# Handing out the late gathers at the planner's own end, two more PSUM banks for odd transform halves, and expert activations laid over the tables

## The chip, the cores and the metric

The kernel runs on one core of one Trainium2 chip. The metric is device time in microseconds (us) of one execution; lower is better. The engines are named as the profile names them: PE (TensorE matmul), PEld (its weight loads), DVE (VectorE), ACT (ScalarE), POOL (GpSimd) and SP (SyncE, which only issues DMAs here).

## The reference

The input `x` has 8 batches of 2496 tokens with 256 values. The first half is the real part of a Fourier transform over tokens and values. The second half sends each of the 19968 rows of that result to one of eight experts, each of which takes at most N // E = 2496 rows, in the order of falling gate values, and applies the expert's two layers.

```python
X = np.fft.fft(np.fft.fft(x, axis=1), axis=2).real.astype(np.float32)
x = X.reshape(B * S, D)                      # N = 19968 rows, D = 256
logits = x @ w_gate                          # E = 8 experts
for idx in np.argsort(-logits.flatten()):    # greedy: highest logit first
    tok, e = idx // E, idx % E
    if assigned[tok] < 0 and counts[e] < N // E:
        assigned[tok] = e; counts[e] += 1
for e in range(E):                           # F = 1024 hidden values
    out[assigned == e] = np.maximum(x[assigned == e] @ w1[e], 0.0) @ w2[e]
```

## The kernel before, in words

The work runs in four stages on one core, and the order of the instructions on PE, DVE, ACT and POOL is the order in which the program emits them (`manual_schedule`).

**Loading and folding.** Rows are loaded, folded with their mirror image and turned; cosine and sine tables `hi` and `lo` are made in the pool `tabs`; the gate's logits come out of the same tables.

**Transforms.** `transform(n)` runs for n = 0 to 19, in two units each: the even half (r = 0), which ACT copies to `ev`, and the odd half (r = 1). A `combine` then adds and subtracts the two on DVE into a stage buffer, ACT and POOL fill in the mirrored quarters, and SP stores the buffer to `t_dram`. The combine of transform n is kept in the list `pending` and emitted in the even unit of transform n + 1. Both halves take their PSUM from `big_ps`, three banks of the tag `h`, which the weight products `wps` (`turn_w`) and the sort products `sps` (`sort_call`) use as well. Two more banks have the tags `t` and `o`; until the experts start, only `first_strips` and the row sums use them. Between the units runs `first_chain`: the first search for the gate's thresholds (`choose`, `lowest`, `search`, `first_strips`), on DVE with short products on PE. It fixes early strips of rows that surely belong to an expert. A small clock (`clock["PE"]`, `clock["D"]`) decides how many units are emitted between two steps of the chain.

**Experts.** `experts` runs iterations j over 40 early tiles (5 strips by 8 experts, 384 rows) and 16 late tiles (8 experts by two). Iteration j has three parts; each emits a third of `up` of tile j (first layer, `hps` to the hidden tile `hb`, L1218) and a third of `down` of tile j - 1 (second layer, `ops`, L1241, then a scatter to the output by POOL, L1245). PSUM results are moved by `take`, which gives each move to ACT or DVE by the running sums `busy`. The list `aside` holds further steps for a part: weights, sort marks, sort products, reloads.

**Rounds.** Beside the early tiles runs `settle_rest`, the rest of the assignment: the end of round 1, three more rounds (each `choose`, `lowest`, three turns of `search`, `settle`), then slots, keys, eight chunks of `inverse` and `decode`, which gives the row numbers of the late tiles. It is a generator: each `yield` names the DVE time of what was just emitted, and `yield SYNC` marks a place where a product on PE follows. At the end of each part `pace` adds 1.9 to its credit, never above 1.9, and emits steps until the credit is spent or a SYNC comes. `place_all`, at iteration 25 part 1, emits all that is left at once. The gathers of the late tiles (POOL, L1194) are put at fixed iterations, 25 + 3m // 2 for late tile m and not before 32 from m = 8 on. When `settle_rest` has ended, `swap_ps` gives the banks of the rounds to the experts, and `widen` gives the buffers `wa` and `dd` to the ring of output tiles.

When the transforms are done, `swap_sb` closes the pool of the stage buffers (`stg`) and that of the tables (`tabs`), which lie next to each other, and opens one pool `deep` over both, for the hidden tiles `hb`, the odd strips `xs`, the gathered rows `xg`, their turned copies `xt` and a ramp `ramp8`.

If the rounds left a token unsettled, a fallback runs after the experts.

Of the kernel before, what the change touches and what calls it, by code (L numbers as in the profile page):

```python
# [52 lines left out]
CB = 20  # L53
KC = 64
OT = 8
SYNC = None
MARK = 1048576.0

# [9 lines left out]
def kernel(  # L68
# [424 lines left out]
    def big_ps(nm):  # L493
        return spread_ps("h", 3, [P, 512], FT, nm)
# [12 lines left out]
    def swap_sb():  # L507
        stg_cm.__exit__(None, None, None)
        tabs_cm.__exit__(None, None, None)
        deep["sb"] = ctx.enter_context(tc.tile_pool(name="deep", bufs=1, side="right"))  # L510

    def work_tile(shape, dt, tag, bufs):
        return deep["sb"].tile(shape, dt, tag=tag, bufs=bufs, name=tag)


    wa = asg.tile([P, E, GC], FT, name="wa")
# [284 lines left out]
        nc.vector.tensor_tensor(kk, kk, none, op=AL.add)  # L801
        nc.vector.scalar_tensor_tensor(rows, in0=bb, scalar=float(S // 2), in1=kk, op0=AL.mult, op1=AL.add)

    ramps = {}
# [12 lines left out]
    def first_strips():  # L817
        low, wid, lo0 = found["low"], found["wid"], found["lo0"]
        lev = small("lev")
        nc.vector.scalar_tensor_tensor(lev, in0=wid, scalar=-0.01, in1=low, op0=AL.mult, op1=AL.add)  # L820
        moved = small("moved")
        nc.vector.tensor_tensor(moved, low, lo0, op=AL.is_gt)
        nc.vector.tensor_scalar(moved, in0=moved, scalar1=2.0 * T_FREE, scalar2=-T_FREE, op0=AL.mult, op1=AL.add)
        fits = small("fits")
        nc.vector.tensor_scalar(fits, in0=exc, scalar1=0.5, scalar2=2.0 * T_FREE, op0=AL.is_lt, op1=AL.mult)
        nc.vector.tensor_scalar(fits, in0=fits, scalar1=-T_FREE, scalar2=None, op0=AL.add)
        nc.vector.scalar_tensor_tensor(lev, in0=lev, scalar=moved, in1=fits, op0=AL.min, op1=AL.max)
        yield 0.8
        yield SYNC
        bps = psm.tile([P, 512], FT, tag="o", bufs=1, name="lev_ps")  # L830
        nc.tensor.transpose(bps[:, 0:P], lev.to_broadcast([P, P]), identf)
# [7 lines left out]
        yield SYNC  # L839
        v = asg.tile([P, GC], FT, tag="sl_v", bufs=1, name="sl_v")  # L840
# [24 lines left out]
        yield 5.5  # L865
        early["t"] = (v, t1, t2, t3)

    def strip_places():
# [125 lines left out]
    td_v = t_dram.rearrange("(n p f) d -> n p f d", p=P, f=8)  # L994
    NB = 2

    pending = []

    def transform(n):
        b0, kc = NB * (n // NK), n % NK  # L1000
        ks = slice(kc * P, (kc + 1) * P)
        st = stg.tile([P, NB, 4, D], BF, tag="stage", bufs=4, name="stage")
        ps = []
        for r in range(2):
            fps = big_ps("fftps").rearrange("p (b d) -> p b d", b=NB)
            for d0, d1, tab in ((0, P + 1, hi["c" + "EO"[r]]), (P + 1, D, hi["s" + "EO"[r]])):
                for i in range(NK):
                    nv = rows_of(i, r)
                    nc.tensor.matmul(fps[:, :, d0:d1], lhsT=tab[:nv, i, ks],  # L1009
                                     rhs=zball[:nv, b0:b0 + NB, 2 * i + r, d0:d1],  # L1010
                                     start=(i == 0), stop=(i == NK - 1))
            ps.append(fps)
            if r == 0:
                ev = stg.tile([P, NB, D], FT, tag="ev", bufs=2, name="ev")
                nc.scalar.copy(ev, fps)  # L1015
            cost = 0.0
            while pending:
                cost += pending.pop(0)()
            yield cost

        def combine():
            nc.vector.tensor_tensor(st[:, :, 0, :], ev, ps[1], op=AL.add)  # L1022
            nc.vector.tensor_tensor(st[:, :, 3, :], ev, ps[1], op=AL.subtract)  # L1023
            for q in range(2):
                nc.scalar.activation(st[:, :, 1 + q, P + 1:D], st[:, :, 3 * q, P + 1:D], ACT.Copy, bias=0.0,  # L1025
                                     scale=-1.0)
                nc.gpsimd.tensor_copy(st[:, :, 1 + q, 0:P + 1], st[:, :, 3 * q, 0:P + 1])  # L1027
            nc.sync.dma_start(td_v[n].rearrange("p f d -> p (f d)"), st.rearrange("p b q d -> p (b q d)"))
            if n < 3:
                reload(n)  # L1030
            return 1.3

        pending.append(combine)


    def turn_w(e, eng=None):
# [105 lines left out]
        clock["D"] = max(clock["D"], clock["PE"]) + 0.3  # L1142
        clock["PE"] = max(clock["D"], clock["PE"])
    for n in range(4):
        sort_mark(n)
        unit()
        sort_call(n, (0, 1), "A")
        unit()
        sort_call(n, (2, 3), "A")
        unit()  # L1150
        reload(n + 3)
        if n == 0:
            strip_places()
        if n == 1:
            payloads(0, payr)
    sort_rows(0, 0)
    while unit():
        pass
    while pending:
        pending.pop(0)()  # L1160
    swap_sb()
    ramp8 = deep["sb"].tile([P, P, 8], BF, name="ramp8")
    ramps[8] = ramp8
    nc.gpsimd.tensor_copy(ramp8, rampw[:, 0:P, None].to_broadcast([P, P, 8]))
    busy["A"] = busy["D"] = 0.0
# [85 lines left out]
    def experts(tiles, group, aside, ahead=0, pace=None):  # L1251
# [4 lines left out]
        for j in range(len(tiles) + 1):  # L1256
            if ahead and j + ahead < len(tiles):
                gather(tiles[j + ahead])
            for part, (fcs, b0) in enumerate((((0, 1, 2), 0), ((3, 4, 5), P), ((6, 7), 2 * P))):
# [6 lines left out]
                if j > 0:  # L1266
                    down(tiles[j - 1], b0, group)
                if pace is not None:
                    pace()
# [12 lines left out]
    for t in range(1, NT):  # L1282
# [6 lines left out]
                at(j + 1, 2, lambda n=n: reload(n + 3))  # L1289
        at(8 * t - 4, 1, lambda t=t: sort_rows(t, 0))  # L1290
        at(8 * t - 1, 0, lambda t=t: sort_rows(t, 1))
    G0 = 25
    for m, d in enumerate(late):
        d["m"] = m
        j = G0 + (3 * m) // 2 if m < 5 else max(32, G0 + (3 * m) // 2) if m >= 8 else G0 + (3 * m) // 2
        at(j, 1, lambda d=d: (place_all(), gather(d)))

    todo = settle_rest()
    placed = []
# [82 lines left out]
```

## Time and profile before

| what | us |
|---|---|
| median of 3 runs | 612.94 |
| lowest and highest of them | 610.62 and 614.84 |
| the profiled execution, its own time | 607.89 |
| its span, from the first to the last instruction | 606.0 |

The profile describes the one execution of 607.89 us. Its page gives busy time per engine, the span in 40 slices, and the chain of work that ended last. The trace behind it answers further questions: busy time in chosen stretches (with the clock that TensorE was granted, 1.00 being full speed), who waited for whom, and instructions in order of time. In rows of the stretches each engine's busy time has its count of instructions in brackets. In rows of the timeline the bracket at the end is the engine's idle time before the instruction and what ended it. In rows of waits the numbers are the total in us, how often, and the longest.

### The profile page before, as it was taken

The numbers are of one execution on the slowest core, as the hardware profiler recorded it, in microseconds if no ns is written. First come the engines' busy times: TensorE is split into PE (matmuls) and PEld (weight loads), VectorE is DVE, ScalarE is ACT, GpSimd is POOL, SyncE is SP. The second block draws the span as 40 slices with busy tenths as digits, with TensorE's granted clock in tenths as the row PEclk, the third lists the DMA queues.
The fourth block names the chain that finished last, engine by engine and source line by source line (L and its number), as shares of the span: only waits on it lengthen the run. The fifth ranks groups of instructions, "written<-read, shape, count | busy, mean of one in ns | idle before, by whom it ended". The sixth has DMA issues, their size and how long they took to land.

```text
span 606.0 us, 11341 instructions
## 1 busy us (share of the span) xinstructions
PE 491.7 (81%) x4023; PEld 363.0 (60%) x4023; DVE 391.4 (65%) x1074; ACT 340.7 (56%) x775; POOL 314.6 (52%) x362
## 2 busy tenths in 40 slices
PE   0577688886978999998999987889687679768994
PEld 0444447755755667776776765557455456556773
DVE  7799865958584878989679898335324234334551
ACT  7889851553656877876777762335323234334551
POOL 7888541622314544644444443566674665665554
PEclk9998999999897999998999997889997898997998
DMA  8999762684697984222222321122221221221111
GB/s 278 305 281 298 226 101 41 222 260 125 164 298 133 165 156 144 98 98 84 96 95 85 94 93 62 55 67 65 73 64 59 65 73 55 58 69 47 60 65 48
DMA packets 35169, 74.63 MB, mean 123 GB/s; under 512 B 6115, under 2 KB 14349, under 8 KB 35104
## 3 DMA queue, kind: packets, MB, share of 16 engines
q0 software_dynamic: 23296, 42.10, 27.3%
q1 hardware_dynamic: 11808, 31.73, 15.7%
q8 instruction: 33, 0.54, 0.4%
q14 instruction: 32, 0.26, 0.1%
HBM read 51.26 MB, written 32.24 MB: 138 GB/s over the span
## 4 chain that ended last, share of the span: by engine, by line
PE 62%; DVE 16%; issue 10%; ACT 8%; POOL 2%; another core or an unknown queue 1%; DMA 1%; POOLq 0%; DVEq 0%; ACTq 0%; SPq 0%
PE hps L1218 22%; PE ops L1241 20%; PE fftps L1009 4%; PE sps L1082 3%; PE tp L284 3%; PE wps L1042 2%; POOL out_dram L1245 2%; DVE pt L1060 2%; ACT zt L286 1%; PE yps L294 1%; DVE stage L1023 1%; PE tp L1206 1%; ACT tf L253 1%; DMA t_dram<-stage 1%
## 5 line engine op out<-in xcount | busy, mean ns | idle before, releaser
L985 ACT ACTIVATE hb<-hps 128x384 bf16<-128x384 f32 (+1 forms) x331 | 147.5, 491 | 93.0 <-PE hps L1218 68.4
L1241 PE MATMUL ops<-w2t,hb 128*128 128x256 bf16 (+1 forms) x1344 | 183.1, 282 | 0.8 <-issue 0.8
L1241 PEld LDWEIGHTS <-hb 128*128 128x128 bf16 (+1 forms) x1344 | 136.5, 102 | 38.5 <-issue 4.3
L1218 PE MATMUL hps<-xs,zball 128*128 128x384 bf16 x640 | 136.9, 341 | 27.3 <-issue 16.6
L1245 POOL DMA_INDIRECT out_dram<-zball,rid x95 | 98.6, 1038 | 109.5 <-ACT zball L985 88.8
L1218 PEld LDWEIGHTS <-zball 128*128 128x128 bf16 x896 | 88.5, 101 | 93.1 <-issue 54.7
L989 DVE TENSOR_SCALAR hb<-hps 128x384 bf16<-128x384 f32 (+1 forms) x117 | 63.3, 547 | 78.0 <-PE hps L1218 43.3
L1218 PE MATMUL hps<-xt,zball 128*128 128x384 bf16 (+1 forms) x256 | 51.3, 330 | 14.6 <-issue 10.7
L128 POOL DMA_INDIRECT xb<-in_x_dram,mir_i x40 | 55.2, 1380 | 11.9 <-issue 11.1
L985 ACT ACTIVATE zball<-ops 128x256 f32<-128x256 f32 x86 | 33.1, 384 | 36.3 <-PE ops L1241 23.5
L284 PE MATMUL tp<-identf,xa 128*128 128x128 f32 x160 | 27.5, 336 | 21.0 <-issue 12.2
L985 ACT ACTIVATE xs<-sps 128x384 bf16<-128x384 f32 x71 | 31.6, 489 | 20.0 <-PE hps L1218 11.3
L284 PEld LDWEIGHTS tp<-identf,xa 128*128 128x128 f32 x160 | 23.2, 174 | 28.6 <-issue 13.1
L1027 POOL COPY stage<-stage 128x258 bf16<-128x258 bf16 x40 | 17.6, 444 | 39.0 <-DVE stage L1022 35.8
L1082 PE MATMUL sps<-pt,xl 128*128 128x192 bf16 x320 | 34.6, 248 | 1.2 <-DVE stage L1023 0.7
L991 DVE COPY zball<-ops 128x256 f32<-128x256 f32 (+1 forms) x32 | 13.5, 423 | 33.3 <-PE ops L1241 12.5
L1060 DVE TENSOR_SCALAR pt<-rampw,spot 128x193 bf16<-128x193 bf16 x160 | 32.4, 294 | 0.0
L1194 POOL DMA_INDIRECT xg<-t_dram,ids_l x24 | 23.5, 978 | 14.9 <-DVE wa L781 7.9
L1082 PEld LDWEIGHTS <-xl 128*128 128x128 bf16 x320 | 28.0, 99 | 4.5 <-issue 1.4
L1245 POOL DMA_INDIRECT out_dram<-zball,rows_l x23 | 22.3, 970 | 15.2 <-DVE zball L991 7.6
L1015 ACT COPY ev<-fftps 128x512 f32<-128x512 f32 x20 | 11.6, 581 | 25.8 <-PE fftps L1009 16.9
L1025 ACT ACTIVATE stage<-stage 128x254 bf16<-128x254 bf16 x40 | 15.8, 414 | 14.1 <-DVE stage L1022 12.4
(358 smaller groups left out, 797.2 us busy)
## 6 DMA issues: line engine op xcount, KB each, us to landing
t_dram<-stage SPq DMA_DIRECT2D x20, 512.0 KB
xl<-t_dram SPq DMA_DIRECT2D x20, 512.0 KB
xa<-in_x_dram SPq DMA_DIRECT2D x8, 1024.0 KB
w1raw<-in_moe_w_dram POOLq DMA_DIRECT2D x8, 512.0 KB
w2t<-in_moe_w_dram POOLq DMA_DIRECT2D x8, 512.0 KB
xa<-in_x_dram SPq DMA_DIRECT2D x8, 224.0 KB
out_dram<-zball,rid POOLq DMA_INDIRECT x95
xb<-in_x_dram,mir_i POOLq DMA_INDIRECT x40
```

The costliest lines, as they stand in the source:

```text
L128: nc.gpsimd.indirect_dma_start(out=bv[0:n, i, :], out_offset=None, in_=x_pairs, in_offset=bass.IndirectOffsetOnAxis(ap=mir_i[0:n, b * NK + ...
L284: nc.tensor.transpose(tp[:, blk, u, :], pv[:, 4 * c + u, blk * P:(blk + 1) * P], identf)
L985: nc.scalar.activation(dst, src, ACT.Relu if relu else ACT.Copy)
L989: nc.vector.tensor_scalar(dst, in0=src, scalar1=0.0, scalar2=None, op0=AL.max)
L1009: nc.tensor.matmul(fps[:, :, d0:d1], lhsT=tab[:nv, i, ks], rhs=zball[:nv, b0:b0 + NB, 2 * i + r, d0:d1], start=(i == 0), stop=(i == NK - 1))
L1027: nc.gpsimd.tensor_copy(st[:, :, 1 + q, 0:P + 1], st[:, :, 3 * q, 0:P + 1])
L1060: nc.vector.tensor_scalar(marks[n][:, f, 0:EW + 1], in0=rampw[:, 0:EW + 1], scalar1=spot[:, c:c + 1], scalar2=None, op0=AL.is_equal)
L1082: nc.tensor.matmul(sps[:, j2 * EW:(j2 + 1) * EW], lhsT=xl[:, 2 * g + cc, j2 * P:(j2 + 1) * P], rhs=pt[:, 2 * g + cc, 0:EW], start=(cc == 0 ...
L1194: nc.gpsimd.indirect_dma_start(out=xg[0:nr, q, :], out_offset=None, in_=t_dram, in_offset=bass.IndirectOffsetOnAxis(ap=d["ids"](q, nr), ax ...
L1218: nc.tensor.matmul(hps[:, 0:n], lhsT=w1t[d["e"]][:, j2, fc * P:(fc + 1) * P], rhs=d["x"](j2), start=(j2 == 0), stop=(j2 == 1))
L1241: nc.tensor.matmul(ops[0:nr, 0:D], lhsT=d["hid"][:, fc, b0:b0 + nr], rhs=w2t[d["e"]][:, fc, :], start=(fc == 0), stop=(fc == F // P - 1))
L1245: put = nc.gpsimd.indirect_dma_start(out=out, out_offset=bass.IndirectOffsetOnAxis(ap=d["rows"](b0 // P)[0:nr], axis=0), in_=ot[0:nr, :], ...
```

## The change

- Odd halves of the transforms take their PSUM from the banks `t` and `o`, in turn, instead of from `h`. So that `first_strips` can use these banks, it emits pending combines (`flush`) before its two groups of products. A combine is put into `pending` at the end of its odd unit; it is still emitted in the next even unit, unless a flush comes first.
- The first sort mark is emitted at the end of `first_strips`, and each further one a step sooner.
- The pool `deep` becomes two: `deepa` with the hidden tiles and odd strips, `deepb` after it with the rest.
- `pace` keeps up to 3.0 of credit.
- `place_all` is gone. When `pace` meets the end of `settle_rest` in iteration j, `settled(j)` widens the ring and swaps the banks; `feed` then hands out gather m at iteration j + 1 + 3m // 2 (from m = 8 on not before 32), at the latest at 38 + m. If the rounds have not ended by iteration 35, `feed` emits the rest at once.

```diff
+CREDIT = 3.0
...
-        deep["sb"] = ctx.enter_context(tc.tile_pool(name="deep", bufs=1, side="right"))
+        deep["sb"] = ctx.enter_context(tc.tile_pool(name="deepa", bufs=1, side="right"))
+        deep["sb2"] = ctx.enter_context(tc.tile_pool(name="deepb", bufs=1, side="right"))
...
-        return deep["sb"].tile(shape, dt, tag=tag, bufs=bufs, name=tag)
+        return deep["sb" if tag in ("hb", "xs") else "sb2"].tile(shape, dt, tag=tag, bufs=bufs, name=tag)
...                                   # first_strips, before lev_ps and before the rps products
         yield SYNC
+        flush()
...                                   # first_strips, at its end
-        yield 5.5
+        sort_mark(0)
+        yield 7.0
...
+    def flush():
+        cost = 0.0
+        while pending:
+            cost += pending.pop(0)()
+        return cost
...                                   # transform(n)
         for r in range(2):
-            fps = big_ps("fftps").rearrange("p (b d) -> p b d", b=NB)
+            fps = (psm.tile([P, 512], FT, tag="to"[n % 2], bufs=1, name="fftps") if r else big_ps("fftps")).rearrange(
+                "p (b d) -> p b d", b=NB)
...
-            cost = 0.0
-            while pending:
-                cost += pending.pop(0)()
+            cost = flush()
+            if r == 1:
+                pending.append(combine)
             yield cost
...                                   # after the loop, before
-        pending.append(combine)
...
     for n in range(4):
-        sort_mark(n)
+        if n < 3:
+            sort_mark(n + 1)
...
-    ramp8 = deep["sb"].tile([P, P, 8], BF, name="ramp8")
+    ramp8 = deep["sb2"].tile([P, P, 8], BF, name="ramp8")
...
-    G0 = 25
     for m, d in enumerate(late):
         d["m"] = m
-        j = G0 + (3 * m) // 2 if m < 5 else max(32, G0 + (3 * m) // 2) if m >= 8 else G0 + (3 * m) // 2
-        at(j, 1, lambda d=d: (place_all(), gather(d)))
...
-    def place_all():
-        if not placed:
-            placed.append(len(list(todo)))
-            widen()
+    def settled(j):
+        placed.append(j)
+        widen()
+        swap_ps()
+
+    def feed(j):
+        m = len(fed)
+        if m < len(late) and not placed and j >= 35 + m:
+            for c in todo:
+                busy["D"] += 0.0 if c is SYNC else c
+            settled(j)
+        while m < len(late) and placed and j >= min(max(placed[0] + 1 + (3 * m) // 2, 0 if m < 8 else 32), 38 + m):
+            gather(late[m])
+            fed.append(j)
+            m += 1
+
+    for j in range(len(tiles) + len(late) - 1):
+        at(j, 1, lambda j=j: feed(j))
...
-    def pace():
-        credit[0] = min(credit[0] + 1.9, 1.9)
-        while credit[0] > 0.0:
+    def pace(j):
+        credit[0] = min(credit[0] + 1.9, CREDIT)
+        while credit[0] > 0.0 and not placed:
             c = next(todo, "end")
             if c == "end":
-                if not placed:
-                    placed.append(0)
-                    widen()
-                if deep["ps"] is None:
-                    swap_ps()
+                settled(j)
                 return
```

More of the change, by code (lines that the diff above doesn't have):

```diff
@@ L802, in decode @@
         nc.vector.scalar_tensor_tensor(rows, in0=bb, scalar=float(S // 2), in1=kk, op0=AL.mult, op1=AL.add)
-    ramps = {}
+    ramps, pending = {}, []
     def index_pair(nm, w):
@@ L839, in first_strips @@
         yield SYNC
+        flush()
         v = asg.tile([P, GC], FT, tag="sl_v", bufs=1, name="sl_v")
@@ L1003, in transform @@
         ps = []
-        for r in range(2):
-            fps = big_ps("fftps").rearrange("p (b d) -> p b d", b=NB)
[L1006 to L1015, printed above, removed]
-            cost = 0.0
-            while pending:
-                cost += pending.pop(0)()
-            yield cost
         def combine():
@@ L1031, in combine @@
             return 1.3
-        pending.append(combine)
+        for r in range(2):
+            fps = (psm.tile([P, 512], FT, tag="to"[n % 2], bufs=1, name="fftps") if r else big_ps("fftps")).rearrange(
+                "p (b d) -> p b d", b=NB)
+            for d0, d1, tab in ((0, P + 1, hi["c" + "EO"[r]]), (P + 1, D, hi["s" + "EO"[r]])):
+                for i in range(NK):
+                    nv = rows_of(i, r)
+                    nc.tensor.matmul(fps[:, :, d0:d1], lhsT=tab[:nv, i, ks],
+                                     rhs=zball[:nv, b0:b0 + NB, 2 * i + r, d0:d1],
+                                     start=(i == 0), stop=(i == NK - 1))
+            ps.append(fps)
+            if r == 0:
+                ev = stg.tile([P, NB, D], FT, tag="ev", bufs=2, name="ev")
+                nc.scalar.copy(ev, fps)
+            cost = flush()
+            if r == 1:
+                pending.append(combine)
+            yield cost
     def turn_w(e, eng=None):
@@ L1158 @@
         pass
-    while pending:
-        pending.pop(0)()
+    flush()
     swap_sb()
-    ramp8 = deep["sb"].tile([P, P, 8], BF, name="ramp8")
+    ramp8 = deep["sb2"].tile([P, P, 8], BF, name="ramp8")
     ramps[8] = ramp8
@@ L1268, in experts @@
                 if pace is not None:
-                    pace()
+                    pace(j)
     tiles = [early_tile(t, e) for t in range(NT) for e in range(E)]
@@ L1291 @@
         at(8 * t - 1, 0, lambda t=t: sort_rows(t, 1))
-    G0 = 25
     for m, d in enumerate(late):
         d["m"] = m
-        j = G0 + (3 * m) // 2 if m < 5 else max(32, G0 + (3 * m) // 2) if m >= 8 else G0 + (3 * m) // 2
-        at(j, 1, lambda d=d: (place_all(), gather(d)))
     todo = settle_rest()
-    placed = []
-    def place_all():
-        if not placed:
-            placed.append(len(list(todo)))
-            widen()
+    placed, fed = [], []
+    def settled(j):
[14 more added lines that the diff above has]
+        at(j, 1, lambda j=j: feed(j))
     credit = [0.0]
-    def pace():
-        credit[0] = min(credit[0] + 1.9, 1.9)
-        while credit[0] > 0.0:
+    def pace(j):
+        credit[0] = min(credit[0] + 1.9, CREDIT)
+        while credit[0] > 0.0 and not placed:
             c = next(todo, "end")
             if c == "end":
-                if not placed:
-                    placed.append(0)
-                    widen()
-                if deep["ps"] is None:
-                    swap_ps()
+                settled(j)
                 return
```

1 line of the change is left out of this document (removed).

## The prediction

> **What bounds the kernel now.** The page comes first: span, busy shares, and the shares of the chain that ended last.
>
> ```profile
> span 606.0 us, 11341 instructions
> ...
> PE 491.7 (81%) x4023; PEld 363.0 (60%) x4023; DVE 391.4 (65%) x1074; ACT 340.7 (56%) x775; POOL 314.6 (52%) x362
> ...
> PE 62%; DVE 16%; issue 10%; ACT 8%; POOL 2%; another core or an unknown queue 1%; DMA 1%; POOLq 0%; DVEq 0%; ACTq 0%; SPq 0%
> ```
>
> PE holds 62% of the chain, DVE 16%. An 81% busy PE is not one limit, so the span is cut into stages: transforms (to 177.49), expert iteration 0, the iterations with the rounds (to 350.14), iterations 24 and 25 (to 374.64), and the late ones.
>
> ```profile
> core 0: us, PE busy (x) PEld busy (x) DVE busy (x) ACT busy (x) POOL busy (x), PEclk, DMA share, GB/s
> 108.00:144.00 36.00, 30.68 (x246) 23.88 (x246) 28.00 (x69) 19.41 (x43) 13.20 (x27) 1.00 0.74 234
> 144.00:177.49 33.49, 28.84 (x255) 22.07 (x254) 24.78 (x74) 19.57 (x46) 7.77 (x18) 0.95 0.65 193
> 177.49:188.56 11.07, 5.66 (x29) 3.37 (x27) 3.83 (x17) 4.73 (x11) 2.85 (x4) 0.71 0.60 155
> 241.38:350.14 108.76, 103.81 (x872) 78.02 (x869) 91.42 (x325) 81.99 (x203) 51.36 (x49) 0.98 0.29 96
> 350.14:374.64 24.50, 18.67 (x162) 14.57 (x160) 21.94 (x68) 10.87 (x26) 8.88 (x10) 0.86 0.20 61
> 374.64:550.00 175.36, 138.32 (x1020) 99.29 (x1018) 65.95 (x152) 64.64 (x144) 108.37 (x111) 0.91 0.20 64
> ```
>
> In the rounds PE is busy 103.81 of 108.76 us and DVE 91.42: both near full. In 350.14 to 374.64 DVE is busy 21.94 of 24.50 and PE has 6 us idle at a clock of 0.86. Idle PE is paid twice: the clock falls after a stop.
>
> **The change part by part.** First the transforms. An odd half held one of three h banks until its combine; now it has t or o, and h serves even halves, weights and sort products alone. Who stopped PE, from 108 to 144 and from 144 to 177.4, then what the clock and DVE did:
>
> ```profile
> PE fftps L1009 <- DVE stage L1023: 2.6, 4, 1.6
> PE wps L1042 <- DVE stage L1023: 1.4, 1, 1.4
> PE lev_ps L831 <- DVE s_lev L827: 1.3, 1, 1.3
> ...
> PE wps L1042 <- DVE stage L1023: 2.5, 1, 2.5
> PE sps L1082 <- DVE stage L1023: 0.7, 1, 0.7
> ...
> 151.48:154.89 3.41, 3.41 (x18) 2.38 (x17) 0.00 (x0) 1.85 (x5) 1.47 (x3) 0.50 0.63 137
> ...
> 155.69 0.69 DVE L1022 TENSOR_TENSOR stage<-ev,fftps 128x512 bf16<-128x512 f32 x1 [4.89 <-PE fftps L1009]
> 156.90 1.69 DVE L1060 TENSOR_SCALAR pt<-rampw,spot 128x193 bf16<-128x193 bf16 x8
> ```
>
> Stops put to L1023, the last reader of an odd half, make 2.6+1.4+2.5+0.7 = 7.2 us, and the 3.41 us at clock 0.50 lose 1.7: 8.9 at most. I take 4. DVE carries both the combines and the first chain, so PE arriving sooner waits for DVE at lev_ps; the two new flushes put one combine each (two adds of 0.69) ahead of the level and the ranks, where the same two combines ran a little later anyway, at 0 to 1.4 us. Behind lev_ps and the ranks on PE wait the next halves and the weight products. The first sort mark (1.69) moves into the chain; the 4.89 us of idle DVE at 155.69 covers it, and without that cover it costs its 1.69. After the flushes, the combine's scalings on ACT still stand ahead of the weight copies, so the 2.5 us stop may stay. Bounds: +3 (flushes and mark uncovered, no stop saved) and -7 (the stops without the dip). The combine's store and reload on SP and its copies on POOL keep their order.
>
> Second, the border. Hidden tiles and the odd strip (24.6 KB a partition) now lie in a pool of their own over the tables (25.6 KB), not over the stage buffers.
>
> ```profile
> 178.10 5.15 DMA t_dram<-stage
> ...
> 183.51 3.15 ACT L985 ACTIVATE hb<-hps 128x384 bf16<-128x384 f32 x6 [5.47 <-DMA t_dram<-stage]
> ...
> PE hps L1218 <- ACT hb L985: 5.4, 1, 5.4
> ...
> 182.20:189.03 6.83, 4.98 (x21) 3.02 (x21) 0.14 (x1) 4.20 (x9) 2.76 (x3) 0.50 0.50 63
> ...
> 183.57 1.04 POOL L1164 COPY ramp<-rampw 128x1024 bf16<-128x1024 bf16 x1 [5.99 <-DMA t_dram<-stage]
> 184.56 1.77 POOL L338 DMA_DIRECT2D w2t<-in_moe_w_dram  x2
> ```
>
> The first eviction waited for the last store. PE stopped 5.4 us, and its 4.98 us of work at clock 0.50 lost 2.5: 7.9. What is late next is ACT: the tile's eight evictions at 3.15/6 = 0.53 us take 4.2 us, against 2.5 for PE's work at full clock, so up to 1.7 of the gain stays with ACT. I take 1.4 off, so -6.5, bounds -5.4 and -7.9. The ramp copy still waits on POOL, and behind it the two w2 loads. They were issued at 184.56 for iterations 2 and 3 (read by the second product, one iteration on); they move 4 us up with the store, their readers 10.5. Three iterations of at least 6 us lie between, so some 11 us remain, against 5.15 for a store of the same 512 KB: covered.
>
> Third, the block at iteration 25. The old code emitted five of the eight inverse chunks and the decode there at once. Sixteen L1218 matmuls make an iteration, so their windows give its length:
>
> ```profile
> 247.35:253.37 6.02, 3.23 (x17) 1.54 (x17) 1.00 0.47 153
> ...
> 350.14:358.47 8.33, 3.16 (x16) 1.51 (x16) 1.00 0.20 66
> 358.47:374.64 16.17, 4.27 (x16) 1.89 (x17) 0.79 0.20 58
> ...
> 367.16 0.64 PE L759 MATMUL inv_ps<-o_eq,oh 128*128 128x48 bf16 x8 [1.04 <-DVE o_eq L755]
> ...
> 369.51 0.21 DVE L776 TENSOR_SCALAR wa<-inv_ps 128x48 int32<-128x48 int32 x1 [0.73 <-PE inv_ps L759]
> ...
> 374.89 0.21 DVE L802 SCALAR_TENSOR_TENSOR rows_l<-wa 128x48 int32<-128x48 f32 x1
> ```
>
> Iteration 25 is 10.15 us over an ordinary 6.02, iteration 24, with paced chunks in all three parts, 2.31: -12.5 if both become ordinary. I counted both schedules from the code's own cost numbers: old, chunk products 3 to 7 land together at iteration 25 (the rows show that block); new, the chunks are handed out from iteration 20 part 2 to 23 part 0, the decode in 23 part 2, and the end is met at 24 part 0. The chunks are then paid paced: 2.31/3 = 0.77 a part, eight parts, +6.2; bounds 8 x 0.33 (a third of the 1.04 stop, if expert work hides the rest) = +2.6 and 8 x 1.04 = +8.3. The decode (369.51 to 375.10, 5.6 us of DVE) holds up no PE instruction but evictions given to DVE, and the planner counts its 3.0 as DVE time and sends them to ACT: +0.5, bounds 0 and 2.
>
> Fourth, the gathers. With the end at 24, gather m comes at 25 + 3m//2, from 8 on not before 32: the old list to the iteration. Ring and PSUM swap come one iteration sooner, at nothing. So the late stretch should stay:
>
> ```profile
> 443.11:448.44 5.33, 3.20 (x16) 1.56 (x16) 1.00 0.20 62
> ...
> PE hps L1218 <- issue: 27.3, 12, 3.4
> ```
>
> An undisturbed late iteration is 5.33 us; 12 stops of 27.3 us in 375 to 606, with POOL 108.37 of 175.36 busy, are there before and after.
>
> Fifth, the credit. A cap of 3.0 keeps credit past a stop, so the same rounds fit fewer parts: three whole rounds need 42 parts where they took 51, 14 iterations for 17.
>
> ```profile
> L690 DVE COPY tsel<-misc x4: 166/166/168, 195.5 to 315.6; 128x8 f32<-128x8 f32 x4
> ...
> 195.65:315.57 119.92, 117.17 (x955) 86.01 (x954) 98.57 (x340) 91.66 (x221) 60.07 (x58) 0.99 0.47 118
> ...
> PE misc L689 <- DVE s_tnew L684: 1.9, 1, 1.9
> PE misc L689 <- DVE trun L685: 0.8, 1, 0.8
> ...
> DVE s_hi L631 <- PE lt L626: 2.3, 3, 0.8
> ...
> 277.77:281.19 3.42, 3.42 (x15) 2.00 (x14) 3.32 (x8) 1.94 (x5) 0.00 (x0) 0.50 0.48 156
> ```
>
> L690 ends a round: three rounds in 119.92. Of that PE lost 2.75 idle and 1.7 at clock 0.50 (after the 1.9 stop). Without three iterations PE needs 119.92-4.45-18.06 = 97.4; DVE needs its 98.57 less about 2.5 of marks. Two engines with equal work and five handovers a round (lists, three searches, settle) cannot hide all waits: at half of s_hi's 2.3/3 = 0.77 each, 15 handovers are 5.8, and with one clock dip of 1.7 the new idle is 7.5, so +3. Bounds: -4.4 (no stop left) and 15 x 0.8 = +12. Behind a late DVE queue the sort marks and the evictions that the balance gives it, and then PE for want of a bank; that is inside the upper bound.
>
> Sum: -4 -6.5 -12.5 +6.2 +0.5 +3 = -13.3. The span goes from 606.0 to 592.7, the profiled execution from 607.89 to 594.6; it lay 0.8% under the median of 612.94, so by that ratio 599.5; I say **600**.
>
> One rule against a row. After the 1.9 and 2.5 us stops above, the clock read 0.50. The Trainium skill (TensorE: Matmul & The Clock Gate, Part 1: The HAM clock gate) has the clock halved only after an idle window of about 3.4 us. By that rule these stops cost their length alone; the ceiling of the first term would be 1.7 lower, and a total lowered in step 601.7. The rows show dips after shorter stops, so I follow them.
>
> **The rivals.** *Packing eats the gain*: 15 handovers at the 0.8 us stop instead of my 5.8+1.7, and chunks at 1.04: +4.5+2.1, and with nothing from the banks +4: 611. For it: PE and DVE both near full. Against: DVE idles 21 of 119.92 us now. *The border stays*: if the new pool still waits for the store, +6.5, 606.5; the sizes speak against. *Slower*: the denser rounds make stops of the 1.9 us kind, each followed by a dip, 1.9+1.7 = 3.6 us. Six such stops among the 15 round handovers add 22 to my 600: 622. That is the point from which it is over 1% slower than before; the trace had one in three rounds. By the skill's rule a stop would cost 1.9 and it would take ten. *Better still*: chunks at 2.6, no new idle, banks 7: 13.3+3.6+3+3 = 23 gained, 590.
>
> **How the numbers follow.** About 1% (6.1 us) is what a measurement can tell from no change. Forecast 0.66 (591 to 606.8); packing 0.14; border 0.08, half of it past 606.8; slower 0.05; better still 0.07. Faster 0.66+0.07+0.04 = 0.77, same 0.18, slower 0.05. The range, 589 to 612, leaves out the slower case and the ends of the unknown costs.
>
> **What would show it.** Right: no ACT wait for t_dram<-stage at the first eviction and no dip at iteration 0; no L1023 stops; eight spread L759 groups; iteration 25 near 6 us; first xg gather still in iteration 25; the late stretch still about 231 us. Wrong: a row of clock 0.50 stretches before iteration 24, L690 still 40 us apart, or a late stretch that changes by more than 5 us, for which I have no term.

## The result and the profile after

The kernel after takes **596.13 us** (median of 4 runs, 593.28 to 599.41); the kernel before took 613.89 us beside it (4 runs, 610.62 to 616.36). The ratio is 0.9716, interval 0.9640 to 0.9792. The forecast was 600, range 589 to 612. The profiled execution took 593.28 us; its page:

```profile
span 591.5 us, 11322 instructions
...
PE 482.5 (82%) x4014; PEld 358.1 (61%) x4023; DVE 383.4 (65%) x1063; ACT 341.7 (58%) x786; POOL 310.8 (53%) x362
...
PEclk9998779999999999999999799999998989989997
```

Of the tenths of the clock, the only 7 between the loading and the last slice is the 23rd (of 14.8 us each), 325 to 340: one new dip. For the stages, first four stretches of the kernel before that the prediction cut otherwise (transforms, iterations 1 to 20, 21 to 23, 26 to the end), then the kernel after (transforms, iteration 0, 1 to 20, 21 to 23, 24 and 25, 26 to the end). Columns as before: window and length, busy time of PE, PEld, DVE, ACT and POOL, clock.

```profile
101.30:177.49 76.19, 65.19 (x550) 50.77 (x550) 59.14 (x164) 40.17 (x91) 25.24 (x60) 0.98 0.63 196
188.56:329.50 140.94, 136.96 (x1105) 100.19 (x1104) 117.76 (x405) 106.97 (x260) 68.39 (x66) 0.99 0.48 120
329.50:350.14 20.64, 19.58 (x183) 14.74 (x181) 17.91 (x63) 15.29 (x38) 8.31 (x9) 1.00 0.31 101
374.64:606.00 231.36, 185.56 (x1402) 136.14 (x1399) 90.30 (x201) 89.19 (x195) 136.42 (x140) 0.91 0.19 62
```

```profile
102.80:173.79 70.99, 62.02 (x546) 49.55 (x551) 59.41 (x164) 39.66 (x91) 25.25 (x60) 1.00 0.68 210
173.79:177.67 3.88, 3.87 (x26) 2.25 (x26) 3.68 (x16) 3.88 (x11) 0.22 (x1) 1.00 0.95 325
177.67:321.06 143.39, 136.76 (x1105) 99.92 (x1110) 124.72 (x439) 109.91 (x269) 68.75 (x68) 1.00 0.48 121
321.06:350.45 29.39, 23.99 (x242) 18.96 (x240) 21.97 (x64) 16.23 (x39) 9.84 (x9) 0.88 0.22 72
350.45:362.92 12.47, 11.97 (x98) 9.11 (x96) 5.07 (x27) 10.43 (x26) 6.46 (x7) 1.00 0.31 102
362.92:591.50 228.58, 181.13 (x1402) 133.67 (x1399) 87.87 (x198) 88.20 (x196) 138.00 (x142) 0.95 0.20 63
```

| stage | before | after | change | forecast |
|---|---|---|---|---|
| loading | 101.3 | 102.8 | +1.5 | 0 |
| transforms (banks) | 76.2 | 71.0 | -5.2 | -4 |
| iteration 0 (border) | 11.1 | 3.9 | -7.2 | -6.5 |
| iterations 1 to 20 (denser rounds) | 140.9 | 143.4 | +2.5 | +3 |
| iterations 21 to 23 (chunks, decode) | 20.6 | 29.4 | +8.8 | +6.2 and +0.5 |
| iterations 24 and 25 (the block) | 24.5 | 12.5 | -12.0 | -12.5 |
| 26 to the end | 231.4 | 228.6 | -2.8 | 0 |
| span | 606.0 | 591.5 | -14.5 | -13.3 |

The gain sits where two waits went: the border and the banks, 12.4 together. The loading, in which the change edits nothing, was 1.5 longer in this trace, so that iteration 0 starts 3.7 us sooner (173.79 for 177.49). The block at iteration 25 is gone too, but of its 12.0 us the stages ahead of it took 11.3 back. The one stop of iterations 21 to 23, and then what DVE did ahead of it:

```profile
328.46 0.64 PE L761 MATMUL inv_ps<-o_eq,oh 128*128 128x48 bf16 x8 [5.40 <-DVE o_eq L757]
```

```profile
325.25:332.07 6.82, 3.60 (x22) 2.63 (x23) 6.13 (x15) 1.85 (x4) 0.00 (x0) 0.50 0.16 43
```

```profile
314.59 0.32 DVE L949 MAX8 keys<-sl_v 128x8 f32<-128x160 f32 x1
...
318.38 1.56 DVE L1071 TENSOR_SCALAR pt<-rampw,spot 128x193 bf16<-128x193 bf16 x8
...
323.83 0.95 DVE L1110 TENSOR_TENSOR bt<-rampw,spot_hi 128x768 bf16<-128x768 bf16 x1
...
326.66 0.69 DVE L751 TENSOR_TENSOR oh<-ramp,l_lo 128x1024 bf16<-128x1024 bf16 x1 [0.20 <-issue]
```

From the first key step (314.59) to the first chunk (326.66) DVE works 12 us with hardly a pause: the keys, a sort mark, the row marks of strip 3 (322.77 to 324.78), the decoding of the keys. PE, whose next instruction in its order is the first chunk's product, waits 5.40 us for that chunk's `o_eq`; the clock is at 0.50 for 6.82 us, in which 3.60 us of PE's work lose half, 1.8, beside what of the stop lies in it. In the kernel before these pieces lay apart, the row marks 18 us ahead of the keys:

```profile
325.55 0.29 DVE L1095 TENSOR_TENSOR a<-iota,spot_lo 128x128 bf16<-128x128 bf16 x1
...
343.64 0.32 DVE L944 MAX8 keys<-sl_v 128x8 f32<-128x160 f32 x1
```

All eight chunks follow in the kernel after; their first and last start stand in this view of the tile:

```profile
L761 PE MATMUL inv_ps<-o_eq,oh x64: 186/220/242, 328.5 to 348.9; 128*128 128x48 bf16 x64
```

### The profile page after: what moved, and what is told of

It is laid out like the page before. It is cut to its first block, busy times and chain, and to the rows that moved or that the text cites. A ratio compares the mean times of both kernels' runs of the same rounds, so it can differ in the third digit from the quotient of the medians.

```text
span 591.5 us, 11322 instructions
## 1 busy us (share of the span) xinstructions
PE 482.5 (82%) x4014; PEld 358.1 (61%) x4023; DVE 383.4 (65%) x1063; ACT 341.7 (58%) x786; POOL 310.8 (53%) x362
## 5 line engine op out<-in xcount | busy, mean ns | idle before, releaser
L990 ACT ACTIVATE hb<-hps 128x384 bf16<-128x384 f32 (+1 forms) x331 | 145.8, 492 | 77.1 <-PE hps L1229 61.0
L1252 PE MATMUL ops<-w2t,hb 128*128 128x256 bf16 (+1 forms) x1344 | 178.1, 277 | 0.1
L1252 PEld LDWEIGHTS <-hb 128*128 128x128 bf16 (+1 forms) x1344 | 134.3, 100 | 35.2 <-issue 1.9
L1256 POOL DMA_INDIRECT out_dram<-zball,rid x94 | 96.2, 1024 | 109.6 <-ACT zball L990 96.2
L1229 PE MATMUL hps<-xs,zball 128*128 128x384 bf16 x640 | 131.5, 330 | 19.3 <-issue 10.5
L1229 PEld LDWEIGHTS <-zball 128*128 128x128 bf16 x896 | 86.6, 99 | 87.0 <-issue 48.2
L990 ACT ACTIVATE zball<-ops 128x256 f32<-128x256 f32 x96 | 36.9, 385 | 46.8 <-PE ops L1252 26.0
L129 POOL DMA_INDIRECT xb<-in_x_dram,mir_i x40 | 53.0, 1326 | 14.0 <-issue 10.8
L990 ACT ACTIVATE xs<-sps 128x384 bf16<-128x384 f32 x73 | 32.4, 493 | 20.0 <-PE sps L1093 11.5
L996 DVE COPY zball<-ops 128x256 f32<-128x256 f32 (+1 forms) x21 | 8.9, 423 | 30.0 <-PE ops L1252 9.6
L287 ACT COPY zt<-tp 128x1024 f32<-128x1024 f32 (+1 forms) x24 | 20.2, 868 | 6.1 <-PE tp L285 6.1
```

What stands on the lines that cost most here:

```text
L129: nc.gpsimd.indirect_dma_start(out=bv[0:n, i, :], out_offset=None, in_=x_pairs, in_offset=bass.IndirectOffsetOnAxis(ap=mir_i[0:n, b * NK + ...
L287: nc.scalar.copy(zt[:, :, 0:nn, :], tp[:, :, 0:nn, :])
L990: nc.scalar.activation(dst, src, ACT.Relu if relu else ACT.Copy)
L1229: nc.tensor.matmul(hps[:, 0:n], lhsT=w1t[d["e"]][:, j2, fc * P:(fc + 1) * P], rhs=d["x"](j2), start=(j2 == 0), stop=(j2 == 1))
L1252: nc.tensor.matmul(ops[0:nr, 0:D], lhsT=d["hid"][:, fc, b0:b0 + nr], rhs=w2t[d["e"]][:, fc, :], start=(fc == 0), stop=(fc == F // P - 1))
L1256: put = nc.gpsimd.indirect_dma_start(out=out, out_offset=bass.IndirectOffsetOnAxis(ap=d["rows"](b0 // P)[0:nr], axis=0), in_=ot[0:nr, :], ...
```

## The experiments

The first eight kernels and the last two ran on chips where the kernel before takes about 559 us, not 614; two ran where it takes 606. So each total is compared with the kernel before on its own chip. No trace of the kernel before comes from a chip of the 559 sort: up to iteration 25 its stages are taken from the trace at 614, and the late stretch is compared only between runs of one sort of chip.

**The border alone.** The kernel before with the pool `deep` in two:

```diff
-        deep["sb"] = ... name="deep" ...
+        deep["sb"] = ... name="deepa" ...
+        deep["sb2"] = ... name="deepb" ...
```

> The kernel before with one part alone: hidden tiles and odd strips in a pool over the tables. Theory (each part pays where it stands and what it gains is kept): the first eviction no longer waits for t_dram<-stage, iteration 0 takes about 4 us instead of 11.1, its clock dip goes, and iteration 26 starts 7 us sooner (367 to 369 instead of 374.6); about 607 us against 614. Rival (the rounds on DVE set the pace up to iteration 25, so what PE gains at the border is given back): iteration 0 is short all the same, but iteration 26 starts less than 3 us sooner; 611 to 614 us.

Measured: 552.06 us against 558.89, ratio 0.9877 (0.9852 to 0.9903). Iteration 0 of its windows, and 26 to the end:

```profile
177.40:181.30 3.90, 3.83 (x27) 2.21 (x26) 3.69 (x16) 3.90 (x11) 0.05 (x1) 1.00 0.87 290
...
366.70:550.70 184.00, 167.64 (x1402) 130.18 (x1400) 92.48 (x203) 91.23 (x195) 136.41 (x140) 0.97 0.24 78
```

The wait for the store is the pool's overlay alone: with it go the stop and the clock dip, and all of the 6.8 us reaches the end.

**The banks alone.** The kernel after with the single pool `deep`, the old `place_all` and `pace`, the old credit.

> The kernel before with another part alone: odd transform halves in the banks t and o, with the two flushes and the earlier sort marks. Theory: the time from the first transform product to iteration 0 falls from 76.2 to about 71 us (the changed kernel has 71.0), the stops put to the combine's last add go except for the weight products', the border wait and iteration 25 stay as before; about 609 us. Rival (the first chain on DVE sets this stage, the banks only move PE's idle time): 75 to 76 us, no change in the total.

Measured: 555.03 us, ratio 0.9939 (0.9924 to 0.9954), 3.9 us by the medians. Transforms, then iteration 0 with the border's wait back in it:

```profile
101.20:172.30 71.10, 62.05 (x547) 49.62 (x552) 59.50 (x164) 39.70 (x91) 25.21 (x60) 1.00 0.68 210
172.30:183.30 11.00, 4.90 (x25) 3.01 (x25) 3.84 (x17) 4.25 (x11) 2.95 (x4) 0.69 0.52 147
```

**The credit alone.** The kernel before with

```diff
-        credit[0] = min(credit[0] + 1.9, 1.9)
+        credit[0] = min(credit[0] + 1.9, 3.0)
```

> The kernel before with one constant changed: the credit's cap 3.0 instead of 1.9. The rounds then end by themselves at iteration 24, one before the block would come, and the gathers stay at their iterations. Theory (the block's 10 us at iteration 25 are paid back in denser rounds: DVE work is the same, fewer iterations of PE work cover it): iterations 24 and 25 near 6 us each, iterations 1 to 23 together 8 to 12 us longer, a stop of about 5 us ahead of the first inverse chunk; iteration 26 starts 0 to 5 us sooner; 609 to 614 us. Rival (the block is pure loss): iterations 1 to 23 as before, 10 us gained or more, 604 us or less.

Measured: 560.37 us, ratio 1.0038 (1.0021 to 1.0055): slower, by 1.5 us in the medians. Iterations 1 to 20, 21 to 23, 24 and 25:

```profile
185.40:328.90 143.50, 136.80 (x1105) 99.73 (x1109) 124.86 (x437) 110.18 (x269) 67.42 (x65) 1.00 0.47 119
328.90:359.00 30.10, 24.89 (x242) 19.42 (x241) 21.91 (x64) 16.33 (x39) 10.08 (x9) 0.89 0.21 70
359.00:371.50 12.50, 12.00 (x98) 9.13 (x97) 5.10 (x27) 10.42 (x26) 6.45 (x7) 1.00 0.31 103
```

The block goes without the new `feed`, and the same two stages pay for it as in the kernel after. DVE's 21.9 us in the block and 17.9 in the stage ahead of it become 5.1 and 21.9, and 117.8 in iterations 1 to 20 become 124.9: the work was moved to where DVE was already busy 84% of the time.

**The old credit in the kernel after.** `CREDIT = 1.9`, so that the rounds end later, at their own pace.

> The changed kernel with the credit's cap back at 1.9: rounds end by themselves at iteration 27, gathers come three iterations later, 28 + 3m//2. Theory (the dense pace is worth about nothing): no 5 us stop ahead of the first chunk and iterations 1 to 20 about 6.7 us each, but chunk parts reach to iteration 26 and the late stretch has the same gathers in fewer iterations; within 3 us of the changed kernel's 596 either way. Rival A (the cap is what pays): 602 us or more. Rival B (the cap costs): 591 or less.

Measured: 548.43 us, ratio 0.9813 (0.9782 to 0.9844). Iterations 21 to 23, 24 and 25, 26 to the end, and what PE waited for in the last:

```profile
315.90:336.70 20.80, 19.57 (x181) 14.72 (x181) 18.05 (x63) 15.29 (x38) 8.34 (x9) 1.00 0.29 100
336.70:352.50 15.80, 14.65 (x139) 11.58 (x137) 14.29 (x40) 10.83 (x27) 6.78 (x7) 1.00 0.26 84
352.50:547.20 194.70, 172.66 (x1427) 132.41 (x1425) 94.21 (x218) 94.70 (x206) 139.04 (x142) 0.95 0.23 74
```

```profile
PE tp L1217 <- DMA xs<-t_dram,ids_l: 5.4, 5, 2.8
```

**The kernel after on that sort of chip**, to set the others against (the same program again):

> The changed kernel once more, beside the kernel before. In the first two profiles the late stretch (iteration 26 to the end) was 231 and 228 us with 14 and 22 stops of PE of some 2.9 us; in the four profiles of the parts it was 184 to 195 us with none, and the kernel before took 559 us there instead of 614. Theory (those stops belong to where a kernel ran, not to the change, and the parts add up: border 0.6 to 1.3%, banks 0.6%, pace about nothing, gathers at the same iterations): where the kernel before takes about 559, the changed one takes 547 to 550, with no such stops; where it takes about 614, 594 to 600. Rival (the stops are of these two kernels): stops and a stretch near 228 us again, whatever the kernel before takes.

Measured: 548.56 us against 558.71, ratio 0.9812 (0.9789 to 0.9835). Its windows for the transforms, 1 to 20, 21 to 23 and 26 to the end:

```profile
101.00:173.60 72.60, 63.83 (x550) 50.39 (x551) 59.41 (x164) 39.64 (x91) 25.19 (x60) 0.98 0.66 205
...
177.50:320.80 143.30, 136.93 (x1109) 99.89 (x1109) 124.60 (x438) 110.03 (x269) 68.55 (x68) 1.00 0.48 122
320.80:350.40 29.60, 24.20 (x243) 19.11 (x242) 21.94 (x64) 16.34 (x39) 10.05 (x9) 0.88 0.22 71
...
362.80:548.00 185.20, 167.62 (x1402) 130.16 (x1400) 91.22 (x198) 91.88 (x196) 137.79 (x142) 0.96 0.25 78
```

So the old credit gives the same total by another way: nothing lost in iterations 1 to 23 (11.5 us less than the kernel after), 3.4 more in 24 and 25, and 9.5 more at the end. There PE is idle for 22.0 us instead of 17.6, because the gathers start later and it waits for those of the last tiles, and busy for 172.66 instead of 167.62; three chunks of the inverse now stand in this stretch. The first gather starts 19 us into iteration 26, in the kernel after (361.0, further down) 2 us ahead of it:

```profile
L1205 POOL DMA_INDIRECT xg<-t_dram,ids_l x24: 911/964/1127, 371.6 to 439.7; - x24
```

The three parts alone multiply to 0.9877 x 0.9939 x 1.0038 = 0.9854; together they are 0.9812, some 2 us better, within what chips and intervals leave open.

**The stop at iteration 21.** If the row marks in the middle of DVE's crowd make it, marking them four iterations sooner takes them out:

```diff
-        at(8 * t - 4, 1, lambda t=t: sort_rows(t, 0))
+        at(8 * t - 8, 1, lambda t=t: sort_rows(t, 0))
```

> The changed kernel with the row marks of a strip (sort_rows part 0, about 2 us of DVE) four iterations earlier, out of iteration 20, where they stand between the keys and the first inverse chunk. Theory (the 5.4 us stop there is DVE work crowded before one handover): the stop falls to 3 to 4 us, iterations 21 to 23 take 25 to 28 us instead of 29.4; the first gather starts as before, because DVE's total is the same; 0 to 3 us less in all. Rival (the stop is the chunks' shared buffers): the stop stays at 5.4 us, no change.

Measured: 549.0 us, ratio 0.9834 (0.9811 to 0.9856), no gain. Iterations 1 to 20, 21 to 23, and the stop:

```profile
176.70:322.10 145.40, 137.07 (x1109) 99.80 (x1109) 126.83 (x443) 110.02 (x269) 69.94 (x68) 1.00 0.48 121
322.10:349.50 27.40, 23.93 (x242) 19.02 (x241) 20.23 (x59) 16.34 (x39) 10.04 (x9) 0.94 0.24 77
```

```profile
PE inv_ps L761 <- DVE o_eq L757: 3.5, 1, 3.5
```

The stop is shorter by 1.9 us and iterations 21 to 23 by 2.2, as the theory had it, and iterations 1 to 20 are longer by 2.1: DVE carries the marks there instead (126.83 for 124.60). PE's idle time there went from 6.4 us to 8.3. So here the sum of DVE's work ahead of the first chunk counts, not its order. The rival in the expectation, shared buffers of the chunks, would have kept the stop at 5.4.

**Gathers one iteration sooner**, and both edits together:

```diff
-        while m < len(late) and placed and j >= min(max(placed[0] + 1 + (3 * m) // 2, 0 if m < 8 else 32), 38 + m):
+        while m < len(late) and placed and j >= min(max(placed[0] + (3 * m) // 2, 0 if m < 8 else 32), 38 + m):
```

> The changed kernel with every gather one iteration sooner: the first in the iteration in which the rounds have ended. Theory (without the 2.9 us stops the late stretch is bound by POOL, whose 48 gathers and some 90 scatters at 1.28 us follow the first gather without a pause): the first gather starts 3 to 6 us sooner and so does the end, 3 to 6 us less than the changed kernel where it has no stops; POOL may wait 1 to 3 us for the row numbers. Rival (PE bounds that stretch): no change within 1 us, the gathers only wait longer to be used.

> The changed kernel with both of these edits. Theory: the two gains add, 4 to 8 us less than the changed kernel where that has no 2.9 us stops. Rival: POOL and PE take turns as the bound, so that the two together give no more than the better one.

Measured: 546.21 us, ratio 0.9777 (0.9753 to 0.9801); both together 546.45, ratio 0.9780 (0.9762 to 0.9797). The sooner gathers are 2.35 us better than the kernel after beside them, less than expected; this is the fastest version. Its end, against the 185.20 above:

```profile
362.00:544.50 182.50, 167.59 (x1402) 130.15 (x1399) 90.98 (x198) 91.86 (x196) 135.74 (x140) 0.97 0.25 79
```

PE's work is the same; what is shorter is the time after it. POOL's last scatter starts at 539.18, where that of the kernel after starts at 542.64; in both the span ends 4.4 us after this scatter has left POOL:

```profile
542.64 0.93 POOL L1256 DMA_INDIRECT out_dram<-zball,rows_l  x1 [0.30 <-DMA out_dram<-zball,rows_l]
```

A second run of that kernel, on a third chip of this sort:

> The kernel of f2_sooner (every gather one iteration sooner) again, beside the same runs of before. Where before takes about 559 us: 546.2 again, ratio 0.975 to 0.980. Where before takes about 606 to 614 us: if the gain of 2.4 us is the last stores' issue ending sooner, 588 to 594 (after: 596 at 613.9, ratio 0.9716); if PE's stops set the late stretch there, no gain can be seen and the ratio stays within 0.964 to 0.979.

Measured: 546.83 us against 559.84, ratio 0.9761 (0.9736 to 0.9785): the same again. Where before takes 606 or more it was not run.

**What sets the end.** The kernel before again, for its trace, and the kernel after with its 48 gathers issued by SP as plain loads (they take rows in order, so the choice of the late rows is left out). Both ran where the kernel before takes 606.06 us.

```diff
-            nc.gpsimd.indirect_dma_start(
-                out=xg[0:nr, q, :], out_offset=None, in_=t_dram,
-                in_offset=bass.IndirectOffsetOnAxis(ap=d["ids"](q, nr), axis=0))
+            nc.sync.dma_start(out=xg[0:nr, q, :], in_=t_dram[(m * 3 + q) * P:(m * 3 + q) * P + nr, :])
```

> The kernel before, unchanged, to have its trace from the chip on which the experiments ran (there it takes about 559 us, against 614 where the prediction was tested). If the 2.85 us stops of PE in the late stretch belong to the place where a kernel runs and not to the kernel, none is in this trace, and iteration 26 to the end takes 184 us as in the parts alone (bounds 182 to 187) against 231.3 in the first trace, while the stages ahead of it stay within 2 us of that trace: border 11.1, iterations 1 to 21 about 140, 24 and 25 about 24.5. If the stops are the kernel's own, they are there again (14 of them) and the time ahead of the late stretch is shorter instead.

> The kernel after, in which the 48 gathers of the late tiles are issued by SP as plain loads of 128 rows in a row instead of by POOL as indirect ones; it leaves out the choice of the late rows, nothing else. In the trace of the kernel after on this chip POOL issues one indirect DMA every 1.28 us from iteration 26 on without a stop, and is still issuing them 15 us after PE's last product. Theory: POOL's queue sets the end of the late stretch, so 48 x 1.28 = 61 us less on it lets PE's pace (30 iterations of 5.22 to 5.9 us, 165 us) and one tail of about 5 us set it: 185 becomes 168 to 173, the kernel 532 to 537 against 548.6. Rival: PE, busy 165.17 of 165.17 us to its last product, sets the end, and POOL's tail is the stores' own time: within 3 us of 548.6.

Measured: the kernel before 611.91 us in one run; with plain loads 551.14 us, ratio 0.9094 (0.9047 to 0.9140). Iteration 26 to the end, of the kernel before and of the plain loads:

```profile
373.80:610.00 236.20, 189.16 (x1402) 136.76 (x1399) 90.42 (x203) 89.09 (x195) 136.17 (x140) 0.89 0.19 61
```

```profile
364.10:549.90 185.80, 167.59 (x1402) 130.12 (x1399) 90.92 (x198) 91.44 (x196) 91.34 (x95) 0.96 0.21 70
```

The trace of before so came from the other sort of chip than its expectation was written for. It shows the slow end of the first trace again, 236.2 us beside 231.4, with stops of PE that have no releaser (rows of waits, iteration 26 to the end):

```profile
PE hps L1218 <- issue: 22.5, 13, 3.4
```

With the gathers off POOL there are none of these; PE's busy time is 167.59 us, within 0.05 us of the kernels at 559. Neither account had that, and it is the larger thing. The kernel after itself was not run on this chip; if it kept its 228.6 us of the trace at 614 here too, some 43 us of the 50 between these two rows hang on the gathers that POOL issues. Against the kernel after at 559 (548.56) the plain loads are 2.6 us longer, so POOL's queue, though it issues without a gap to 542.64 there, does not set the end by tens of us: the theory of 532 to 537 falls. The rival's time (within 3 us) came, but its reason is not shown, for the span runs on 15.4 us after POOL's last scatter, with no engine busy in any row:

```profile
533.59 0.93 POOL L1254 DMA_INDIRECT out_dram<-zball,rows_l  x1 [0.30 <-issue]
```

**Gathers or a dense queue?** The kernel after without the scatters of tiles 25 to 39 (those rows of the output are left out):

```diff
+        if "still" in d:          # set for tiles[25:]
+            return
         put = nc.gpsimd.indirect_dma_start(
```

> The kernel after, in which the output scatters of tiles 25 to 39 (iterations 26 to 40) are not issued; it leaves out those rows of the output, nothing else. POOL so has 45 indirect DMAs less between iteration 26 and 40, about as many as the 48 that went with the gathers in e5_plain (which had none of the 2.85 us stops on a place where the kernel before takes 606 us), and all the gathers stay. Where the kernel before takes about 606 to 614 us: if a dense POOL queue makes the stops (they follow three or four indirect DMAs 1.28 us apart), iterations 26 to 40 have at most 2 of them and the whole lies near 570 (596 less 11 stops of 2.85 with some dips); if the gathers themselves make them, the 11 stops of the kernel after in iterations 26 to 40 stay and it lies above 585. Where the kernel before takes about 559 us no stops are to be lost: 545 to 549, and nothing is told apart.

Measured: 545.34 us against 559.84, ratio 0.9752 (0.9729 to 0.9774). It ran at 559, where nothing is told apart on the stops. It does bound POOL's share of the end there:

```profile
360.90:543.30 182.40, 167.64 (x1402) 130.18 (x1400) 91.25 (x198) 91.86 (x196) 93.03 (x97) 0.97 0.16 48
```

With 45 indirect DMAs less, 182.40 for 185.20: taking away POOL's backlog is worth 2.8 us to the kernel after, and gathers one iteration sooner (182.50) win as much. The rest of the end does not hang on POOL's last scatter: it starts at 530.44 here, 12.2 us sooner than in the kernel after, and the span still runs to 543.3 (548.0 there). What holds the end in this run and in that of the plain loads stays open.

## Why the prediction was right, point by point

**Banks: right** (-4 forecast, -5.2), with some luck. The stops put to the last step of the combine fell from 7.2 us to 2.8, and the dip at 151.48 is not in this trace (clock 1.00 through the transforms). PE's waits in them:

```profile
PE wps L1053 <- ACT zball L990: 3.6, 2, 2.1
PE fftps L1033 <- DVE stage L1017: 2.3, 4, 1.6
...
PE rps L849 <- DVE stage L1017: 0.5, 1, 0.5
```

As feared, a stop ahead of the weight products stayed, now put to ACT. My "no L1023 stops" was too strong. The dip behind that stop is not gone for good either: of ten traces with the new banks, all with this stop of 2.1 us at about 150, four show half clock behind it (the second trace of the kernel after, with 72.6 us of transforms, and those of both edits together, of the second run with sooner gathers and of the plain loads) and six do not. So of the 5.2 us some 1.7 are the dip, which comes and goes.

**Border: right** (-6.5, -7.2). No wait for `t_dram<-stage`, no dip. The 1.4 us that I left with ACT were not there:

```profile
174.32 2.40 ACT L990 ACTIVATE hb<-hps 128x384 bf16<-128x384 f32 x6
```

Six evictions took 2.40 us, 0.40 each, where I had used 3.15/6 = 0.53, a price from the stretch in which PE ran at half clock and its products came more slowly.

**Block and gathers: right.** -12.0 for -12.5; the first gather is in iteration 25, as forecast:

```profile
L1205 POOL DMA_INDIRECT xg<-t_dram,ids_l x24: 915/967/1010, 361.0 to 442.4; - x24
```

**Chunks and decode: the term with the wrong mechanism.** Forecast +6.2 (bounds +2.6 to +8.3) and +0.5 (0 to 2); measured +8.8 for both. The size is not the failure, it lies inside the summed bounds; the mechanism is. I priced eight chunks at 0.77 each, from iterations in which chunks were paced. They came one step later than I counted (first at 328.46, in iteration 21, not in part 2 of 20), and PE's idle time, 29.39 - 23.99 = 5.40 us, is the one stop at the first of them; before it was 1.06. So +8.8 is 4.3 of idle, 1.8 of slow clock and 2.6 of the products' own time on PE: no later chunk stops PE. What I left out is the chain on DVE ahead of the first chunk (keys, marks, decoding, 12 us), which must be done before any of them can start, and whose length the sooner row marks changed together with the stop (5.4 to 3.5). The credit alone (30.10 us in these iterations) and the old credit in the kernel after (20.80) show that the pace brings it here.

**Credit: right in size, but not where the sum put it** (+3, +2.5). Three rounds did take the three iterations less: 119.92 us became 102.6.

```profile
L692 DVE COPY tsel<-misc x4: 155/167/245, 184.3 to 286.9; 128x8 f32<-128x8 f32 x4
```

Within them PE was idle for 4.2 us (102.60 - 98.37), without a dip, not for the 7.5 of the sum; before, stop and dip together had cost 4.45. So of the +2.5 the rounds show 0.7 (102.6 for 97.4 + 4.45), and the rest lies in the iterations around them. And the saving of three iterations bought nothing: alone, the credit costs 0.4%. Its use in the change is that the gathers start sooner, and the old credit with later gathers came out equal.

**The late stretch: within my 5 us** (-2.8), for no reason that I had given. PE's idle time was 45.8 us before and 47.5 after (231.36 - 185.56 and 228.58 - 181.13); the clock, 0.91 and 0.95, makes the difference. At 559 the kernel after has 185.2 there against 184.0 with the border alone. So the -2.8 is not shown to belong to the change. The result's ratio is to be read with that in mind: 0.9716 and 0.9812 overlap only at their ends (0.9640 to 0.9792, and 0.9789 to 0.9835), and of the 1.9% of the second the parts alone give 1.5%.

**The total: close in part by luck.** The chunks and the loading missed by +2.1 and +1.5, the banks, the border and the late stretch by -1.2, -0.7 and -2.8; the misses nearly cancel.

**The rivals.** Packing ate some 11 us of the block's 12, more than I thought, but banks and border paid in full, so 611 was far. The border's wait did not stay. In iterations 1 to 23 a stop with a dip came once, not six times.

**The rule weighed against the rows** (the Trainium skill, TensorE: Matmul & The Clock Gate, Part 1: The HAM clock gate; a drop only after an idle window of about 3.4 us). The new stop of 5.40 us fits the rule and the row alike. A later one does not fit: PE idle 2.04 us, then a stretch at half clock, with PE busy for 1.37 of the 3.41 us ahead of it. The sum's own price, a dip behind every such stop, is not borne out either: behind the 2.1 us stop in the transforms it came in four traces of ten.

```profile
422.58 1.03 PE L1252 MATMUL ops<-w2t,hb 128*128 128x256 bf16 x8
423.47 0.81 PE L1229 MATMUL hps<-xs,zball 128*128 128x384 bf16 x4
426.33 0.48 PE L1229 MATMUL hps<-xs,zball 128*128 128x384 bf16 x2 [2.04 <-ACT hb L990]
```

```profile
427.65:431.06 3.41, 3.41 (x16) 2.02 (x14) 0.56 (x1) 1.37 (x3) 2.73 (x3) 0.50 0.31 111
```

## What to carry to other kernels

A wait that came from which buffer lies over which was worth its stop and the slow clock behind it, and taking it away reached the end in full. Work moved out of a block is not saved by that: count, engine by engine, what the stretch that receives it was already doing, and look for the one chain that must be done before its first result, not for an average price per step. Before a stage is called unchanged, see it on more than one chip.

## What the runs showed of the hardware that was not expected

The kernel before takes 614, 606 or 559 us depending on where it ran. As far as the traces go, the difference lies in the stretch in which POOL issues indirect gathers and scatters, one every 1.27 us where nothing holds them up (0.97 and 0.30 idle): 231.4 and 236.2 us for the kernel before, 228.6 for the kernel after, against 182 to 186 in every version at 559 but the old credit's. Up to that stretch, stages agree within about 2 us. On the slow chips PE stops there for up to 3.4 us with no releaser, and the clock falls behind some of these stops. With the 48 gathers off POOL, on a chip of the slow sort, none of it is seen (185.8). Whether the indirect gathers themselves do it, the rows that they read or the density of POOL's queue, and why only some chips show it, stays open: the run meant to tell them apart came to a chip without the stops.

Whether the clock halves behind a stop of 2 to 3 us is not settled by its length. The same 2.1 us stop of the same product was followed by half clock in four traces and not in six, and the stop of the kernel before at that place in three traces (2.53, 2.53 and 2.74 us) but not in that of the credit alone (2.75 us).
